# A warm-up of TensorE in small tiles, in a retention-and-hardswish kernel on one core

## The chip, the core and the metric

The kernel runs on one core of a Trainium2 chip. The core has TensorE (PE, with its weight loads shown apart as PEld), VectorE (DVE), ScalarE (ACT), GpSimd (POOL) and SyncE (SP), and sixteen DMA engines ("rings" below, one queue's share of a transfer on each). The metric is device time in microseconds of one execution, a median over several. The time before is 289.05 us, the median of three runs from 288.21 to 289.22.

## The reference

Two stages, one after the other. The first is a retention layer: for 8 batches and 8 heads, sequence 576, head size 64,

```python
scores = scale * np.matmul(q, k.transpose(0, 1, 3, 2))
Dmat = np.where(rel >= 0, gamma[:, None, None] ** rel[None, :, :], 0.0)   # rel = s - t, gamma by head
ret = scores * Dmat[None, :, :, :]
attn_out = np.matmul(ret, v)
```

The second takes the 4608 x 512 result as x and runs a feed-forward layer with w_in (512 x 2048) and w_out (2048 x 512):

```python
h = x @ w_in
g = h * np.clip(h + 3.0, 0.0, 6.0) / 6.0
out = g @ w_out
```

Inputs and output are float32; the kernel multiplies in float16 and accumulates in float32.

## The kernel before

The sequence is cut into pieces of 128 positions (four "main" pieces a batch and a shared "rest"). Retention runs piece by piece in chunked form: inside a piece by masked scores (`sc`, then `at` after the mask), across pieces by a state per head (`tbd`, `u`). The result `xt` goes, in blocks of 512 positions, through the first product (`ph`, with `win`), the hardswish on ACT and DVE, and the second product (`pout`, later in seven partial products `x`, `y`, `z`). From about 18 us on TensorE works through these products, with the retention of later pieces between them.

The order of the instructions on each engine is the order in which the program issues them (a manual schedule); engines meet by semaphores only. Everything that this change touches is at the beginning:

- SP loads q of pieces 0 and 1 in float32 (`load_q`, L123). POOL's queue then takes k and v of pieces 0 and 1, then q, k, v of pieces 2 and 3 (all L102), then `win` (L129) and `wout` (L134). These loads change float32 to float16 on the way, in packets of 128 bytes. Each transfer is split over sixteen rings, and a consumer waits for all sixteen parts.
- DVE sets up constants: `zeros` (L148, 128 x 512 float16), `cb` (L150, L151), the decay tables, the identity, and `dq` (L174), a diagonal matrix with the decay.
- TensorE starts with the warm-up: matmuls of `zeros` by `zeros` whose results nobody reads (`warm`, L215). Seven have 512 columns and two have 128. They write banks of the ring of four PSUM banks tagged `ph`.
- Then `q_by_pe(0)` (L265) brings q of piece 0 into transposed form with the decay (it needs ACT's cast of q, L126), `warm(2, MBLK)` follows, `k_by_pe(0)` (L256) transposes k, and `warm(6, P)` follows.
- For pieces 0 to 3 (the `EARLY` ones) come: scores (L341, the last piece L283), mask on DVE (L345, the last piece L286), the state (L314, L318 on TensorE, L323 on DVE), the output (L359 and L370, the last piece L297 and L303). `scale_v` (L245, DVE) scales v of each piece ahead of the state's matmul L314.
- The first block's first product starts behind piece 3's output with L600 (halves of 256 columns) and goes on with L574 (512 columns).

TensorE's and the other engines' instructions come from memory themselves; the profile shows their transfers as queues of the kind "instruction" (q8 in packets of 16 KB, q14 in packets of 8 KB).

The warm-up as it stands, and its call:

```python
    def warm(n, cols):
        w = bank([P, MBLK], FP32, name=f"warm_{warmed[0]}")
        warmed[0] += 1
        for _ in range(n):
            nc.tensor.matmul(w[:, 0:cols], zeros[:, 0:P], zeros[:, 0:cols],
                             start=True, stop=True)

    warm(7, MBLK)
    warm(2, P)
```

Of the kernel before, what the change touches and what calls it, by code (L numbers as in the profile page):

```python
# [10 lines left out]
FP32 = mybir.dt.float32  # L11
FP16 = mybir.dt.float16
# [5 lines left out]
def kernel(  # L18
# [16 lines left out]
    nc = tc.nc  # L35
# [3 lines left out]
    P = 128  # L39
    NPAIR = H // 2  # L40
    HALF = P // 2
    NCC = DM // P
    NFC = DFF // P
    MBLK = 512
# [18 lines left out]
    const = ctx.enter_context(tc.tile_pool(name="const", bufs=1))  # L63
# [21 lines left out]
    def bank(shape, dtype, name):  # L85
        return psum.tile(shape, dtype, tag="ph", bufs=4, name=name)
# [8 lines left out]
    def load_third(c, i):  # L95
        if c not in loaded:
            vn = nat.tile([P, H, D], FP16, tag="vn", bufs=NBUF, name=f"vn_{c}")
            qk = nat.tile([P, 2, H, D], FP16, tag="qkn", bufs=NBUF, name=f"qkn_{c}")
            loaded[c] = {"qkn": qk, "q16": qk[:, 0], "kn": qk[:, 1], "vn": vn, "dma": []}
        dst, src = ((loaded[c]["kn"], k), (loaded[c]["q16"], q), (loaded[c]["vn"], v))[i]  # L100
        for p0, b, s0, n in pieces[c][3]:
            loaded[c]["dma"].append(nc.gpsimd.dma_start(  # L102
                dst[p0:p0 + n], src[b, :, s0:s0 + n, :].rearrange("h s d -> s h d")))
# [9 lines left out]
    def load_kv(c):  # L113
        load_third(c, 0)
        load_third(c, 2)
# [28 lines left out]
    load_q(1)  # L144
    load_kv(0)
    load_kv(1)
    zeros = const.tile([P, MBLK], FP16)
    nc.vector.memset(zeros, 0.0)  # L148
    cb = const.tile([P, 2], FP32)
# [51 lines left out]
    for i in range(5):  # L201
# [2 lines left out]
            nc.vector.memset(t, 0.0)  # L204
        tbd.append(t)

    newest = [None]
    warmed = [0]

# [5 lines that stand above are left out]
            nc.tensor.matmul(w[:, 0:cols], zeros[:, 0:P], zeros[:, 0:cols],  # L215
                             start=True, stop=True)

    warm(7, MBLK)
    warm(2, P)

    def make_mask64():
# [8 lines left out]
    free_tbd = list(range(5))  # L230
    state_of = {}
    ts_of = {}

    def rows(i):
        return slice(i * HALF, i * HALF + HALF)

    def run_later(n):
        for _ in range(n):
# [159 lines left out]
    def update_state(c, copies_later=False):  # L398
# [14 lines left out]
        if last:  # L413

            state_of[b] = None
            ts_of[b] = lambda h2, p: ts[rows(h2), p, :]
        else:
            new = free_tbd.pop(0)
            state_of[b] = new
# [19 lines left out]
    def scores4(cs):  # L439
        sc = psum.tile([P, 2, 2, NPAIR, HALF], FP32, tag="sc", name=f"sc_{cs[0]}")  # L440
        at = work.tile([P, 2, 2, NPAIR, HALF], FP16, tag="at", bufs=3, name=f"at_{cs[0]}")
        for j, c in enumerate(cs):
            qk = st[c]["qk"]
            st[c]["at"] = at[:, :, j]
            for p in range(NPAIR):
                for h2 in range(2):
                    for half in range(2):
                        nc.tensor.matmul(sc[rows(half), h2, j, p, :],  # L448
                                         qk[rows(h2), 1, p, rows(half)],
                                         qk[rows(h2), 0, p, rows(half)], start=True, stop=True)  # L450

        def mask():
            if len(cs) == 2:
                nc.vector.tensor_tensor(  # L454
                    out=at.rearrange("t a j p s -> t (a j p) s"),
                    in0=sc.rearrange("t a j p s -> t (a j p) s"),
                    in1=mask64[:, None, :].to_broadcast([P, 4 * NPAIR, HALF]), op=ALU.mult)
            else:
                nc.vector.tensor_tensor(
                    out=at[:, :, 0], in0=sc[:, :, 0],  # L460
                    in1=mask64[:, None, None, :].to_broadcast([P, 2, NPAIR, HALF]), op=ALU.mult)
        return mask
# [626 lines left out]
```

## Time and profile before

| what | value |
|---|---|
| median of three runs | 289.05 us (288.21 to 289.22) |
| profiled execution | 288.14 us |
| its span, first to last instruction | 286.4 us |
| TensorE busy | 277.3 us (97%) |
| DVE, ACT, POOL busy | 227.9, 177.5, 107.2 us |
| warm-up matmuls on the timeline | 1.20 to 4.58 us |
| first matmul of the first product (L600) | 18.11 us |

The span starts with the first instruction and all times below are counted from it; 1.7 us of the execution lie outside. In lines of the timeline the first number is the start, the second the time until the last of the merged instructions ends, and in brackets the idle time before it with what ended it. In the table by stretches, each engine has its busy time and its number of instructions in brackets, then the granted TensorE clock, the DMA share and GB/s. The column of the granted clock has no records for the first microseconds and shows 1.00 there; the spacing of matmuls tells the clock instead.

### The profile page before, as it was taken

What the parts mean: (1) busy time and instruction counts of PE and PEld (TensorE: products, weight loads), DVE (VectorE), ACT (ScalarE), POOL (GpSimd) and SP (SyncE); (2) the same over time, 40 slices, a digit from 0 to 9 for tenths busy, and PEclk for the clock granted to TensorE, in tenths of its full rate; (3) what the DMA queues carried; (4) which work ended last, traced back from release to release, by engine and by line L of the source; (5) the groups of instructions that cost most, each with busy time, mean ns of one, the idle gap of its engine ahead of it and who ended that gap; (6) DMA issues with size and microseconds to landing.
All of it is one profiled execution on the core that took longest, in us unless ns stands there. A gap on an engine that the chain in (4) does not pass through costs nothing.

```text
span 286.4 us, 8439 instructions
## 1 busy us (share of the span) xinstructions
PE 277.3 (97%) x3540; PEld 178.8 (62%) x3540; DVE 227.9 (80%) x376; ACT 177.5 (62%) x313; POOL 107.2 (37%) x134
## 2 busy tenths in 40 slices
PE   7879999999999999999999999999999999999994
PEld 3544445864565597459745884588458845874583
DVE  4948756898768998899879997999799678727861
ACT  6748437875458655865587557755775477358720
POOL 8962669266404332432443434256640000000000
PEclk9999999999999999999999999999999999999999
DMA  9999999999999979998999999999993240121014
GB/s 138 153 195 205 190 160 217 178 151 163 134 169 165 128 81 128 161 150 83 123 172 154 72 132 177 161 78 126 179 157 48 79 108 5 39 76 38 3 37 110
DMA packets 156166, 35.94 MB, mean 125 GB/s; under 512 B 142912, under 2 KB 155072, under 8 KB 156128
## 3 DMA queue, kind: packets, MB, share of 16 engines
q0 software_dynamic: 115760, 18.23, 89.8%
q1 hardware_dynamic: 39920, 16.78, 28.4%
q8 instruction: 27, 0.44, 0.6%
q10 hardware_dynamic: 448, 0.39, 0.4%
q14 instruction: 11, 0.09, 0.1%
HBM read 36.70 MB, written 9.44 MB: 161 GB/s over the span
## 4 chain that ended last, share of the span: by engine, by line
PE 92%; POOL 3%; DMA 2%; DVE 1%; issue 0%; ACT 0%; POOLq 0%
PE ph L574 39%; PE x L712 15%; PE pout L627 10%; PE z L712 9%; PE y L712 4%; PE ph L600 4%; DMA vn<-in_v_dram 2%; POOL qkn L102 2%; PE sc L448 2%; PE o L480 2%; PE o L502 2%; PE u L530 1%; PE xtu L712 1%; PE xo L712 1%; POOL vn L102 1%; PE o L370 1%
## 5 line engine op out<-in xcount | busy, mean ns | idle before, releaser
L574 PE MATMUL ph<-xt,win 128*128 128x512 f16 x520 | 113.7, 379 | 0.0
L582 ACT ACTIVATE u<-ph,cb 128x512 f32<-128x512 f32 x130 | 89.3, 687 | 23.2 <-PE ph L574 23.0
L583 DVE SCALAR_TENSOR_TENSOR gt<-u,ph 128x512 f16<-128x512 f32 x130 | 87.0, 685 | 17.7 <-ACT u L582 16.3
L574 PEld LDWEIGHTS <-win 128*128 128x128 f16 x520 | 50.9, 98 | 59.4
L102 POOL DMA_DIRECT2D qkn<-in_k_dram x40 | 34.0, 850 | 47.6 <-PE ph L600 16.8
L712 PEld LDWEIGHTS <-sum_s 128*128 128x128 f16 x448 | 43.2, 98 | 5.5 <-issue 0.3
L102 POOL DMA_DIRECT2D vn<-in_v_dram x40 | 33.9, 848 | 25.7 <-PE ph L574 10.9
L102 POOL DMA_DIRECT2D qkn<-in_q_dram x38 | 32.1, 845 | 29.9 <-PE ph L574 8.5
L712 PEld LDWEIGHTS <-gt 128*128 128x128 f16 x336 | 32.5, 98 | 5.4
L627 PE MATMUL pout<-wout,gt 128*128 128x512 f16 x128 | 29.1, 379 | 0.0
L680 POOL DMA_DIRECT2D out_dram<-osb x1 | 0.6, 617 | 68.2 <-DVE osb L733 68.2
L712 PE MATMUL x<-wsum_t,sum_s 128*128 128x256 f16 x192 | 22.9, 273 | 0.0
L627 PEld LDWEIGHTS <-gt 128*128 128x128 f16 x128 | 12.0, 98 | 13.5
L330 DVE TENSOR_TENSOR qkn<-qkn,gqk 128x1024 f16<-128x1024 f16 x28 | 19.1, 683 | 0.0
L668 DVE TENSOR_TENSOR sum_s<-gt 128x1024 f16<-128x1024 f16 (+1 forms) x21 | 18.1, 864 | 0.2
L454 DVE TENSOR_TENSOR at<-sc,mask 128x1024 f16<-128x1024 f32 x14 | 17.0, 1217 | 1.1 <-PE sc L448 1.1
L514 ACT CAST xt<-o 64x512 f16<-64x512 f32 x28 | 16.2, 580 | 0.3
L564 DVE TENSOR_TENSOR ta<-u,th 128x256 f32<-128x256 f32 x24 | 10.2, 424 | 5.4 <-ACT th L549 4.4
L712 PE MATMUL z<-wout,sum_s 128*128 128x256 f16 x112 | 13.6, 273 | 0.1
L712 PE MATMUL z<-wsum_t,sum_s 128*128 128x256 f16 x112 | 13.5, 273 | 0.0
L712 PE MATMUL y<-wout,gt 128*128 128x256 f16 x112 | 13.4, 273 | 0.0
L600 PE MATMUL ph<-xt,win 128*128 128x256 f16 x112 | 12.9, 273 | 0.0
(122 smaller groups left out, 304.4 us busy)
## 6 DMA issues: line engine op xcount, KB each, us to landing
out_dram<-osb SPq DMA_DIRECT2D x32, 256.0 KB, 3.6
qkn<-in_k_dram POOLq DMA_DIRECT2D x32, 128.0 KB, 5.1
vn<-in_v_dram POOLq DMA_DIRECT2D x32, 128.0 KB, 5.2
qkn<-in_q_dram POOLq DMA_DIRECT2D x30, 128.0 KB, 5.5
wout<-in_moe_w_out_dram POOLq DMA_DIRECT2D x4, 512.0 KB, 14.8
win<-in_moe_w_in_dram POOLq DMA_DIRECT2D x4, 256.0 KB, 7.6
win<-in_moe_w_in_dram POOLq DMA_DIRECT2D x2, 512.0 KB, 11.2
qf<-in_q_dram SPq DMA_DIRECT2D x2, 256.0 KB, 3.5
```

The source lines that it names most:

```text
L102: loaded[c]["dma"].append(nc.gpsimd.dma_start(dst[p0:p0 + n], src[b, :, s0:s0 + n, :].rearrange("h s d -> s h d")))
L330: nc.vector.tensor_tensor(out=both, in0=both, in1=gqk, op=ALU.mult)
L454: nc.vector.tensor_tensor(out=at.rearrange("t a j p s -> t (a j p) s"), in0=sc.rearrange("t a j p s -> t (a j p) s"), in1=mask64[:, None, ...
L514: nc.scalar.copy(to[rows(h2), :, :, 1, :], o[1][rows(1 - h2)].rearrange("e j p s -> e p j s"))
L564: nc.vector.tensor_tensor(out=ta, in0=st[c]["u"][1], in1=st[c]["sum"], op=ALU.add)
L574: newest[0] = nc.tensor.matmul(ph, win16[:, dmc, P * fc:P * fc + P], xt_of(kb)[:, dmc, :], start=(dmc == 0), stop=(dmc == NCC - 1))
L582: nc.scalar.activation(u, ph, ACTF.Relu, bias=cb[:, 0:1], scale=1.0 / 6.0)
L583: nc.vector.scalar_tensor_tensor(out=gts[kb][:, fc, :], in0=u, scalar=1.0, in1=ph, op0=ALU.min, op1=ALU.mult)
L600: newest[0] = nc.tensor.matmul(ph[:, i], win16[:, dmc, P * (fc + i):P * (fc + i) + P], xt_of(kb)[:, dmc, cols], start=(i == 0 and dmc == 0 ...
L627: nc.tensor.matmul(pout, gt[:, fc, P * mc:P * mc + P], wout16[:, fc, :], start=(fc == 0), stop=(fc == NFC - 1))
L668: nc.vector.tensor_tensor(out=s(which)[:, c0:c1], in0=x(), in1=y(), op=op)
L712: newest[0] = nc.tensor.matmul(dst, left()[:, c, P * u:P * u + P], right[:, c, :], start=(first and c == 0 and (u == 0 or name not in whol ...
```

## The change

A tile `few` of 128 x 64 float16 zeros is set ahead of `zeros`. The seven matmuls of 512 columns give way to 113 small ones and two of 512. A small one multiplies 64 rows of `few` by 64 rows of `few`, 64 columns, and writes one half of the partitions of one of two PSUM banks; four in a row use the four quarters of TensorE's array in turn. The two of 128 columns stay. The helper `rows` moves up in the program unchanged.

```diff
     load_kv(0)
     load_kv(1)
+    few = const.tile([P, HALF], FP16)
+    nc.vector.memset(few, 0.0)
     zeros = const.tile([P, MBLK], FP16)
     nc.vector.memset(zeros, 0.0)
...
+    def rows(i):
+        return slice(i * HALF, i * HALF + HALF)
+
...
-    warm(7, MBLK)
+    def warm_small(n):
+
+        w = [bank([P, MBLK], FP32, name=f"warm_small{x}") for x in range(2)]
+        for i in range(n):
+            x, h = divmod(i % 4, 2)
+            nc.tensor.matmul(w[x][rows(h ^ x), 0:HALF], few[rows(h)], few[rows(h)],
+                             start=True, stop=True)
+
+    warm_small(113)
+    warm(2, MBLK)
     warm(2, P)
...
-
-    def rows(i):
-        return slice(i * HALF, i * HALF + HALF)
```

## The prediction

> **What bounds the kernel now.** I read the page first (busy shares, DMA queues), then the chain of waits, then the timeline of the first 20 us, because the change touches nothing later. The page, shares and DMA queues:
> ```profile
> span 286.4 us, 8439 instructions
> PE 277.3 (97%) x3540; PEld 178.8 (62%) x3540; DVE 227.9 (80%) x376; ACT 177.5 (62%) x313; POOL 107.2 (37%) x134
> ...
> q8 instruction: 27, 0.44, 0.6%
> ```
> TensorE is the bound, and the busy time by stretches says where it is not: 12.01 us busy of the first 16.67, then 29.00 of 29.00.
> ```profile
> 0.00:16.67 16.67, 12.01 (x143) 6.70 (x143) 10.43 (x36) 10.51 (x23) 14.78 (x23) 1.00 1.85 150
> ...
> 84.00:113.00 29.00, 29.00 (x442) 21.11 (x441) 27.15 (x45) 19.76 (x36) 9.97 (x12) 1.00 1.04 118
> ```
> So from the first L600 matmul on, the end follows at a fixed distance, and the change is worth what it does to the start of L600, now 18.11 us. The timeline of the beginning:
> ```profile
> 1.20 3.38 PE L215 MATMUL warm<-zeros 128*128 128x512 f16 x9 [1.20 <-DVE cb L150]
> ...
> 3.93 0.62 ACT L126 CAST qkn<-qf 128x512 f16<-128x512 f32 x1 [1.40 <-DMA qf<-in_q_dram]
> ...
> 4.60 0.64 PE L265 MATMUL trq<-dq,qkn 128*64 128x128 f16 x8
> ...
> 14.47 0.40 PE L283 MATMUL sc<-qk 64*128 64x128 f16 x8
> ...
> 16.20 0.43 DVE L245 TENSOR_TENSOR vn<-vn,gqk 128x512 f16<-128x512 f16 x1 [1.96 <-DMA vn<-in_v_dram]
> ...
> 16.54 1.28 DVE L286 TENSOR_TENSOR at<-sc,mask_wide 128x512 f16<-128x512 f32 x2
> 16.68 0.23 PEld L314 LDWEIGHTS <-qkn 128*128 128x128 f16 x4 [1.99 <-DVE vn L245]
> 16.68 0.40 PE L314 MATMUL u<-vn,qkn 128*128 128x128 f16 x4 [1.82 <-DVE vn L245]
> ```
> (q8: packets, MB, share.) See that the first real work (L265) waits for q's cast, which waits for a DMA, and not for the warm-up; and that TensorE later stands 1.82 us for the scaled v of the fourth piece, whose load is late. The chain of waits and the queues in the 10 ns after 14.10 us:
> ```profile
> 9.35 6.83 DMA vn<-in_v_dram
> ```
> ```profile
> q8 instruction: 1, 0.02, 592.5%
> ```
> That load took 6.83 us where the other early ones took 4.6 to 4.9. In the trace's records fifteen of its sixteen parts had landed by 13.98 us and the last at 16.18; in between, at 14.107, one 16 KB packet of q8 ran for 0.95 us, and the last two packets of v went right after it, at 15.04. q8 moves 27 packets for the 7080 instructions of TensorE (262 each), and this first one starts when 268 of them are counted in the stretch 0 to 14.11 us. I read it as TensorE's own instructions being fetched through a ring that still held v.
>
> **The change, part by part.** *Start of the warm-up.* The small matmuls wait for the memset of `few`, 32 words a partition against 256 for `zeros`. The zeros memset took 0.27 us, one of one word 0.06; in between by size, 0.09 us. TensorE started 0.05 us after the memset, so it starts at 0.87 + 0.09 + 0.05 = 1.01 in place of 1.20. DVE's later setup moves by up to 0.09 us; dq (L174) waits 0.33 us for ACT, which hides it. If not, it would cost at most 0.09.
>
> *113 small matmuls.* The trace has such 64x64 tiles at full clock only:
> ```profile
> 66.61:66.87 0.27, 0.26 (x32) 0.27 (x1) 0.15 (x1) 1.00 1.88 188
> ```
> 32 in 0.27 us, 8.3 ns each, four tiles at a time. The warm-up runs at the slow clock: L215 starts every 0.427 us there against 0.228 at 5.17 us, and the L265 pairs every 0.106 us at 4.60 against 0.056 at 7.85. At 1.9 times, 15.8 ns each, 1.79 us. Bounds: 113 x 8.3 = 0.94 us, and one after another at half of 0.106 us, 6.0 us. I take 1.79, the nearest rows being the same tiles. With two of 0.427 and two of 0.106 (1.07 us) the warm-up ends at 1.01 + 1.79 + 1.07 = 3.87 us, against 4.37 now. L265 waits for the cast that ends at 4.55 either way: no gain. At the upper bound L265 would be 3.5 us late. Bank numbers turn by two in the ring of four; the tiles that they wait for are long done, 0 us.
>
> *Where TensorE's instructions are counted.* 117 matmuls with their weight loads in place of 9 add 216 instructions ahead of everything. What now begins as number 268 at 14.1 us will be number 484; number 268 becomes today's 52, which falls at about 6 to 7 us, and earlier if the issue runs ahead. So the first q8 packet comes in the span 4 to 7 us, and the second at today's number 308, about 17.2 us, behind the wait for v. The late v then has the pace of the other loads: 9.35 + 4.8 = 14.15 us.
>
> *What is late next.* With v there at 14.15, its scaling ends by 14.7, behind DVE's tbd (13.56 + 0.68). The scores at L283 (14.47) then set the pace: L345 follows its scores by 0.44 us, so L286 starts at 14.91 in place of 16.54 and L600 at 18.11 - 1.63 = 16.48 us. That is the most that can be won, 1.63 us. The packet has a price in its new place: 0.95 us on one ring that holds k and v of pieces 0 and 1. Of this k of piece 1 has 0.33 us to spare (landed 7.87, used 8.20), v of piece 0 has 0.15 (its scaling ends at 7.49, and DVE's next step L345 starts at 7.64), k of piece 0 nothing. Each of them starts the chain of DVE and TensorE work that ends at L286, and DVE is busy 3.91 of the 4 us from 8 to 12, so a delay stays: 0.62 to 0.95 us, I take 0.8. From below: nothing, if it falls before 3.9 us, where these queues are empty. From above: the 2.1 us that this packet cost v where it is now, and then 0.5 us are lost, not won. The lag left on v's ring is below the chain's delay. Later packets move by 216 instructions too; the view of waits names none of TensorE's after 18.2 us, so 0.
>
> *The clock.* The L215 rows show it turn between 4.93 and 5.17 us, 4.0 us after the first matmul. I take the same time after the change. TensorE's streaming there falls from 3.17 to 2.86 us and has a pause of 0.7 us ahead of L265, so this can fail. The Trainium skill, "TensorE: Matmul & The Clock Gate", Part 1, says the clock opens after a free-running window of about 3.4 us that was busy; a warm-up with a pause could by it miss one window, and the sum would be that of the second rival below in place of mine. The rows of before neither confirm nor refuse that.
>
> Sum: L600 at 16.48 + 0.8 = 17.3 us, 0.8 us less. The profiled execution took 288.14 us (span 286.4 and 1.7 around it), 0.9 below the median of 289.05 and below all three runs (288.21 to 289.22). From its own time 287.35, from the median 288.25; I say **287.8**, between them.
>
> **The rivals.**
> *Full gain.* The packet runs while the load queues are empty, before about 3.9 us, or in a slack. For it: the small matmuls are issued fast, and the count reaches 236 in the warm-up itself. Against: the first packet today came only at 268. L600 at 16.48: 288.14 - 1.63 = 286.5, or 287.4 from the median.
> *Nothing is won.* The packet costs the early loads its 2.1 us, or the clock needs another 4.0 us: from 5.17 to 9.2 the chain has six groups of 0.21 us (L256 twice, L341, L314, L265, L370) that take as long again, 1.26 us, and L600 starts at 17.3 + 1.26 = 18.56. 288.1 to 288.6; from the median up to 289.5. For it: the ring is at work without a break from 4 to 13 us (148 GB/s) and has little to catch up with. The Trainium skill, "Runtime: NRT & Kernel Launch", "Instruction fetch mechanics", has instructions come in blocks of 256 whose fetch is mostly hidden; by that this case gives 288.14 too. The count of 262 a packet agrees with it; the late v speaks against "hidden".
> *Slower: the clock stays slow into the dense part.* Place: TensorE from 5.17 us. The small tiles and the pause leave the clock closed; the waits up to 14 us may keep it so. Price: 25 groups of 0.21 us up to L600 take 5.3 us more, and with half to all of it on the chain L600 is at 16.48 + 2.65 to 5.3 = 19.1 to 21.8, plus some 2 us for 4 us of L600 and L574 at half speed: 291.1 to 293.8. It decides once over 3.1 us are lost (1.63 of cover and 0.5%). Against: TensorE was busy only 3.81 of the 6 us from 12 to 18, and the clock held.
>
> **How the numbers follow.** A measurement of this kernel tells some 0.5% (1.44 us) from no change, so faster means below 287.6. Forecast case, chance 0.42, 287.2 to 288.4 by its two bases: 0.15 of it faster, 0.27 the same. Full gain 0.20, faster. Nothing won 0.20, the same (it starts at 288.1, and ends 0.2% above the median). Slow clock 0.18, slower. Together faster 0.35, same 0.47, slower 0.18. The range reaches from the full gain (286.5) to short of the slow clock's cases (290.5).
>
> **What would show it.** The first q8 packet at 4 to 7 us and none at 13 to 16; DVE L245 of the fourth piece waiting under 0.5 us near 14 to 15 us; L600 starting at 17.3; L265 still at 4.60; 113 small ones in about 1.8 us; L215 and L256 after 5.2 us at the fast spacing (0.228 and 0.056). The prediction is wrong if the fourth v is late again, if the groups after 5.2 us keep the spacing of 0.106, or if TensorE waits for instructions.

## The result, and the profile after

The changed kernel takes 289.15 us (median of 11 runs, 287.99 to 289.56) against 287.21 for the kernel before (median of 11, 286.72 to 289.22). The ratio is 1.0052, with a 95% interval of 1.0029 to 1.0075: slower by about half a per cent, 0.8 to 2.2 us. The forecast was 287.8 and a small gain over 289.05. The time lies in the stated range of 286.5 to 290.5, but the kernel moved the other way. The three runs that were known of the kernel before (288.21 to 289.22) lie at the upper end of its spread: the eight others of this comparison took 286.72 to 287.39.

In the changed kernel the line numbers behind the warm-up are 11 higher: L265 is L276, L256 is L267, L245 is L256, L600 is L611.

The page of the changed kernel, its span, its instruction queue and the granted clock in 40 slices of 7.2 us:

```profile
span 287.2 us, 8657 instructions
...
PEclk9599999999999999999999999999999999999999
...
q8 instruction: 28, 0.46, 0.7%
```

The second slice, 7.2 to 14.4 us, ran at half clock (the digit of the first slice counts only from the first record, at 3.80 us). The timeline of the changed kernel's beginning (start, time to the end, work, idle time before it and what ended it):

```profile
0.96 1.75 PE L228 MATMUL warm_small<-few 64*64 64x64 f16 x113 [0.96 <-DVE few L148]
...
2.65 1.25 PE L220 MATMUL warm<-zeros 128*128 128x512 f16 x4
...
4.57 0.41 PE L276 MATMUL trq<-dq,qkn 128*64 128x128 f16 x8 [0.68 <-ACT qkn L126]
...
4.92 0.60 PE L220 MATMUL warm<-zeros 128*128 128x512 f16 x2
...
7.43 0.61 PE L267 MATMUL trk<-ident,qkn 128*128 128x128 f16 x4 [1.91 <-DMA qkn<-in_k_dram]
...
17.15 0.41 DVE L256 TENSOR_TENSOR vn<-vn,gqk 128x512 f16<-128x512 f16 x1
...
19.17 1.92 PE L611 MATMUL ph<-xt,win 128*128 128x256 f16 x16
```

The warm-up does what was worked out, and L276 is on time. Then TensorE stands 1.91 us for k of piece 0. The fourth v (the L256 step at 17.15) now waits for nobody. L611 starts at 19.17 us. The queues of the changed kernel in the 10 ns after 3.46 us, and the beginning of its chain of waits:

```profile
q8 instruction: 1, 0.02, 746.2%
```

```profile
1.37 6.02 DMA qkn<-in_k_dram
7.39 0.05 issue
7.43 0.61 PE trk L267 x4
```

The first packet of instructions has moved from 14.1 to 3.46 us, where it runs for 1.19 us. Fifteen of the sixteen parts of k of piece 0 had landed by 5.96 us, the last at 7.39. The last part of each of the next seven loads is 1.4 us behind the fifteenth as well, up to 13.7 us. The profile does not name the ring of a packet; that this one shares a ring with the late part is read from the times. They agree in all fourteen profiles: in the eight whose first packet comes by 5.8 us, k or v of piece 0 has one part that lands 1.2 to 1.8 us behind the fifteenth, and in the six others none of the two is over 0.3 us behind.

The same stage of the kernel before in a second profiled execution, of 286.93 us:

```profile
6.22 0.40 PE L256 MATMUL trk<-ident,qkn 128*128 128x128 f16 x4
...
14.35 0.43 DVE L245 TENSOR_TENSOR vn<-vn,gqk 128x512 f16<-128x512 f16 x1
...
16.69 1.92 PE L600 MATMUL ph<-xt,win 128*128 128x256 f16 x16
```

Its first packet runs from 13.17 us, v of the fourth piece lands at 14.32 all the same, and L600 starts at 16.69, not at 18.11. So the comparison is 19.17 against 16.69, 2.48 us. TensorE's work and clock between k and the first product, by stretches, of the changed kernel and then of the kernel before:

```profile
7.40:19.17 11.77, 11.07 (x141) 7.49 (x142) 8.18 (x12) 6.78 (x14) 10.79 (x15) 0.72 2.01 171
```

```profile
6.22:16.69 10.47, 8.81 (x141) 5.93 (x142) 8.34 (x12) 6.91 (x15) 10.00 (x13) 1.00 2.44 161
```

The same 141 matmuls, busy 11.07 us at a mean clock of 0.72 against 8.81 at 1.00. Of the 2.48 us, 1.21 is the later start of k's transposition (7.43 against 6.22), and 1.27 is the longer way from there (11.74 against 10.47). The dense part gives 0.38 us back (263.87 against 264.25 us from the first L600 or L611 to the last matmul); near 137 us this execution of the kernel before has 0.52 us between two starts of TensorE, and the changed kernel has no such gap. That leaves 2.10; the two executions differ by 2.06 us.

### The profile page after: what moved, and what is told of

It reads as the page before. It is cut to its first block, busy times and chain, and to the rows that moved or that the text cites. A ratio compares the mean times of both kernels' runs of the same rounds, so it can differ in the third digit from the quotient of the medians.

```text
span 287.2 us, 8657 instructions
## 1 busy us (share of the span) xinstructions
PE 278.7 (97%) x3648; PEld 181.0 (63%) x3648; DVE 228.3 (79%) x377; ACT 177.6 (62%) x313; POOL 107.2 (37%) x134
## 4 chain that ended last, share of the span: by engine, by line
PE 91%; DMA 5%; DVE 1%; ACT 1%; issue 0%; POOL 0%; POOLq 0%
PE ph L585 39%; PE x L723 15%; PE z L723 9%; PE pout L638 7%; PE y L723 4%; PE ph L611 4%; DMA qk<-qkn 3%; DMA qkn<-in_k_dram 2%; PE o L513 1%; PE sc L459 1%; PE o L491 1%; PE xtu L723 1%; PE xo L723 1%; PE u L541 1%; PE sc L352 1%; PE trq L276 1%
## 5 line engine op out<-in xcount | busy, mean ns | idle before, releaser
L594 DVE SCALAR_TENSOR_TENSOR gt<-u,ph 128x512 f16<-128x512 f32 x130 | 87.0, 685 | 17.3 <-ACT u L593 16.0
L611 PE MATMUL ph<-xt,win 128*128 128x256 f16 x112 | 12.9, 273 | 0.0
## 6 DMA issues: line engine op xcount, KB each, us to landing
wout<-in_moe_w_out_dram POOLq DMA_DIRECT2D x4, 512.0 KB, 14.9
```

Source lines behind the costliest of these rows:

```text
L594: nc.vector.scalar_tensor_tensor(out=gts[kb][:, fc, :], in0=u, scalar=1.0, in1=ph, op0=ALU.min, op1=ALU.mult)
L611: newest[0] = nc.tensor.matmul(ph[:, i], win16[:, dmc, P * (fc + i):P * (fc + i) + P], xt_of(kb)[:, dmc, cols], start=(i == 0 and dmc == 0 ...
```

## The experiments

Two causes stood against each other: the *transfer* (216 more instructions bring the first packet forward onto the rings that hold k and v) and the *clock* (small tiles and a pause warm TensorE badly). Runs of one group share the runs of the kernel before.

**The changed kernel again.**

> The changed kernel as it is, to see how its start varies. Theory 'transfer': the first 16 KB packet of TensorE's instructions again comes at 3 to 4 us, k of piece 0 lands after 7 us in place of 6.1, and L611 starts near 19 us; 1.0 to 1.9 us over the kernel before. Theory 'clock': the delay is the slow clock; then executions differ with the time at which the clock opens, and one with a clock that stays open from 3.8 us on has L611 before 18 us, with the packet where it is.

Measured: 289.02 us, ratio 1.0057 (1.0036 to 1.0077). Packet at 4.36 us, last part of k at 7.66, L267 at 7.70, L611 at 18.50. The full clock is on record from 4.42 to 7.83 us and again from 11.24. The transfer is confirmed. That L611 comes before 18 us when the clock opens early is not, but the clock did not stay open either: it closed just after the wait for k.

**The count alone.** The full array, as many instructions:

```diff
-    warm(7, MBLK)
+    warm(115, P // 4)
     warm(2, P)
```

> The kernel before with its seven matmuls of 512 columns cut into 115 of 32 columns in the full 128x128 array: the instruction count of the change (234 against 18), about the same columns in all (3680 against 3584), no small tiles. Theory 'transfer': first packet at 3 to 5 us, k of piece 0 about 1.3 us late, +1.0 to +1.5 us as with the change. Theory 'clock': the array is filled as before, so within 0.3 us of the kernel before.

Measured: 288.68 us, ratio 1.0039 (1.0021 to 1.0057). The packet came at 5.80 us, too late to hold k of piece 0 (landed at 6.17, on time); v of piece 0 landed at 8.51, 1.5 us behind its fifteenth part. The waits of this kernel:

```profile
DVE vn L245 <- DMA vn<-in_v_dram: 3.4, 1, 3.4
...
PE u L314 <- DVE vn L245: 1.4, 1, 1.4
```

So the instruction count by itself, with the array as full as before, brings most of the loss (1.3 us over the kernel before, where the changed kernel has 1.7 in the same group), and the rival that wanted 0.3 us at most falls. The clock comes in behind it: it closed from 8.88 to 15.71 us. Five of its ten runs have a mean recorded clock of 0.997 or more and took 287.44 to 288.57 us (mean 287.84); the five at 0.994 or less took 288.80 to 289.42 (mean 289.12). Where no closing is on record, the count costs only half a microsecond here.

**The shape alone.** Small tiles and pause, few instructions:

```diff
-            nc.tensor.matmul(w[x][rows(h ^ x), 0:HALF], few[rows(h)], few[rows(h)],
+            nc.tensor.matmul(w[x][rows(h ^ x)], few[rows(h)], zeros[rows(h)],
                              start=True, stop=True)
-    warm_small(113)
+    warm_small(14)
```

> The changed kernel with its 113 small matmuls of 64 columns merged into 14 of 512 columns in the same 64x64 tiles (the same columns, some 1.6 us, the same pause of about 0.7 us), so 36 instructions of warm-up in place of 234. Theory 'transfer': the first packet stays late (after 11 us), k of piece 0 lands at 6.1 us, within 0.3 us of the kernel before. Theory 'clock': small tiles and pause are the cause, so the clock opens late or closes again and +1.0 to +1.5 us as with the change.

Measured: 288.25 us, ratio 1.0023 (1.0003 to 1.0043). The packet stays at 12.96 us, k lands at 6.28, and L611 starts at 17.16, two microseconds sooner than in the changed kernel, although the clock opened only at 9.48. Neither expectation on the time is met: it is 0.9 us over the kernel before, and half of that comes from somewhere new. The waits of this kernel's TensorE from 136 to 140 us:

```profile
PE o L513 <- issue: 1.2, 1, 1.2
```

In the middle of a burst of small matmuls TensorE stands, with 1.42 us between two starts, and the profile names no engine and no load. A packet of q8 ran from 136.13 to 137.06 us, and TensorE went on 1.4 us after its end. In the kernel before the longest distance of two starts there is 0.36 and 0.52 us in the two profiles, in the changed one 0.20.

**The pause filled.** Four matmuls of 512 columns behind the small ones:

```diff
-    warm(2, MBLK)
-    warm(2, P)
+    warm(4, MBLK)
```

> The changed kernel with four matmuls of 512 columns after the small ones in place of two of 512 and two of 128, so that the pause of 0.7 us ahead of L276 is filled and the count of instructions stays 234. Theory 'transfer': no gain, k of piece 0 is still late, +1.0 to +1.5 us over the kernel before. Theory 'clock': the clock opens and stays open, and the time falls back to the kernel before or under it.

Measured: 288.77 us, ratio 1.0059 (1.0042 to 1.0076). Packet at 4.21, k at 7.62, L611's place at 18.59; the clock open from 6.06 to 9.47 and again from 12.89. Filling the pause wins nothing, though it left some idle time ahead of L276 (0.29 us in place of 0.68). So the pause was not the cause of the loss.

**The kernel before again.**

> The kernel before, unchanged, for a profile of its usual execution (the one shown took 288.1 us, eight later ones 286.7 to 287.4). Theory 'v is usually in time': the first packet of instructions falls beside v of piece 3 without holding it, v lands near 14.2 us and L600 starts near 17 us. Theory 'v is always late': L600 at 18 us, and the later executions are faster for a reason elsewhere.

Measured: 287.60 us, ratio to its own other runs 1.0008 (0.9993 to 1.0024). Its profile is the one shown above: v of piece 3 is in time, and L600 starts at 16.69 us. Over all groups the kernel before has medians of 287.21, 287.37, 287.29 and 287.93 us, with single runs from 286.65 to 290.14; the execution of 288.14 us that the prediction was read from is one of the longer ones. That all the longer ones have a late v is not shown: only these two were profiled.

**The packet sooner.** 16 columns in the small matmuls:

```diff
-            nc.tensor.matmul(w[x][rows(h ^ x), 0:HALF], few[rows(h)], few[rows(h)],
+            nc.tensor.matmul(w[x][rows(h ^ x), 0:16], few[rows(h)], few[rows(h), 0:16],
                              start=True, stop=True)
...
     warm_small(113)
-    warm(2, MBLK)
+    warm(5, MBLK)
```

> The changed kernel with 16 columns in place of 64 in the small matmuls, and five of 512 in place of two after them: the count of instructions is nearly the same (240 against 234), but they are used up faster, so that the first packet should come some 0.7 us sooner, about 2.7 to 3.7 us, when the rings do not yet hold k. Theory 'transfer': the last part of k of piece 0 lands 0.4 to 1.0 us sooner than with the change (6.3 to 7.0), and the time falls by 0.5 to 1.2 us, to 0 to +1.0 us of the kernel before. Theory 'clock': the warm-up is now mostly the old one, so the clock opens and stays as in the kernel before and the time falls by all of it, whatever the packet does.

Measured: 289.12 us, ratio 1.0061 (1.0041 to 1.0081). The edit failed to do what it was for: 113 matmuls of 16 columns take as long as of 64 (the next work starts at 2.60 in place of 2.65 us), and the packet came at 4.51 us. The changed kernel itself has it at 3.46, 4.36 and 3.93 in three profiles, so its place varies by more than the edit was to move it. As a test of the place it says nothing. As a second look at the clock it is clear: k at 7.91, clock closed from 8.62 to 15.45, L611 at 19.74.

**The wait for k filled, first try.** In the changed kernel:

```diff
     q_by_pe(0)
-    warm(2, MBLK)
+    warm(8, MBLK)
```

> The changed kernel with eight matmuls of 512 columns in place of two between L276 and L267, so that TensorE has work while k of piece 0 is late. Theory 'the late k closes the clock, and the slow clock adds to it': k lands late as before, but the clock does not close after it, the groups up to L611 keep the spacing of 0.056 us, and L611 starts 0.5 to 1.0 us sooner than with the change; +0.3 to +1.0 us over the kernel before. Theory 'the late transfer alone': no gain over the change, +1.5 us.

Measured: 288.59 us, ratio 1.0047 (1.0022 to 1.0073). Inconclusive: in the profiled execution the clock opened for the first time at 9.94 us, so the eight matmuls, at half clock, outlasted the wait for k (landed at 7.61), and L267 started only at 8.80. From there to L611 it took 10.29 us, as in the kernel before (10.47).

**The wait for k filled, second try.** The same edit on the kernel with 16 columns:

> The kernel with 16 columns in the small matmuls and five of 512 after them (packet at 4.5 us, L611 at 19.74, clock open at 5.21 and closed again from 8.62 to 15.45), with eight matmuls of 512 columns in place of two between L276 and L267. Theory 'the late k closes the clock, and the slow clock adds to it': the clock opens by 5.2 us and stays open, k still lands near 7.9, and L611 starts at 18.0 to 18.5, the lateness of k alone (1.4 us) over the 16.7 of the kernel before; 0.5 to 1.5 us less than without the fill. Theory 'the late transfer alone': L611 stays near 19.5.

Measured: 287.80 us, ratio 0.9990 (0.9970 to 1.0011), against 1.0061 without the fill. The kernel before had slower runs in this group (median 287.93, elsewhere 287.21 to 287.37), so I compare the profiles. Without the fill, then with it:

```profile
7.95 0.40 PE L267 MATMUL trk<-ident,qkn 128*128 128x128 f16 x4 [1.89 <-DMA qkn<-in_k_dram]
...
19.74 0.50 PE L611 MATMUL ph<-xt,win 128*128 128x256 f16 x3
```

```profile
8.26 0.39 PE L267 MATMUL trk<-ident,qkn 128*128 128x128 f16 x4
...
18.30 1.92 PE L611 MATMUL ph<-xt,win 128*128 128x256 f16 x16
```

With the fill L267 starts 0.31 us later and L611 1.44 us sooner. The clock opened at 7.46 (later than I had expected) and did not close. The way from L267 to L611 is 10.05 us in place of 11.79. All ten runs with the fill have a mean recorded clock of 0.998 or more; without it seven of nine have 0.994 or less. This isolates the second half of the loss in this kernel: the wait for k lets the clock close, and the slow clock stretches the chain behind it.

**Small tiles once more, other places of the blocks.** The kernel with 14 small tiles, and 12 instructions fewer:

```diff
     warm(2, MBLK)
-    warm(2, P)
+    warm(1, 2 * P)
...
-    warm(6, P)
+    warm(1, MBLK)
```

> The 14 small tiles of 512 columns again, with 12 instructions fewer (two of 128 columns become one of 256, the six of 128 ahead of the scores one of 512), so that the blocks of instructions begin nearly where they do in the kernel before (6 later in the count in place of 18). Theory 'the stall of 1.4 us at 138 us came from the place of a block': it is gone, and the time falls by 0.7 to 1.2 us, to within 0.5 us of the kernel before, the rest being the clock that opens late. Theory 'small tiles are dear in themselves': +0.6 us as before.

Measured: 287.92 us, ratio 1.0003 (0.9976 to 1.0030). The time is as expected against the runs of its group (median 287.93, elsewhere 287.21 to 287.37), the reason is not: the stall near 138 us is still there with 1.02 us between starts. The clock opened at 5.02 us this time and L611 started at 16.65. So at the start small tiles cost nothing by themselves when the clock opens in time; the dense part behind is 0.9 us longer than in the second profile of the kernel before (265.17 against 264.25).

**Twelve instructions fewer in the kernel before**, twice:

```diff
     warm(7, MBLK)
-    warm(2, P)
+    warm(1, 2 * P)
...
-    warm(6, P)
+    warm(1, MBLK)
```

> The kernel before with 12 instructions fewer ahead of the first product: the two of 128 columns become one of 256, and the six of 128 ahead of the scores become one of 512. Every block of instructions begins 12 later. Theory 'places of the packets decide': the first packet comes 0.5 to 1 us later, after v of piece 3 has landed, and the time is 0 to 1 us under the kernel before. Theory 'they do not': the same within 0.3 us.

> The kernel before with 12 instructions fewer once more, in more rounds. If the places of the packets decide: first packet after 14.3 us, no stall near 138 us, 0.3 to 0.7 us under the kernel before. If not: the same within 0.2 us.

Measured: 286.87 us, ratio 0.9986 (0.9965 to 1.0008), then 286.68, ratio 0.9958 (0.9939 to 0.9978). The packet comes at 14.74 and 14.99 us, behind the fourth v; L600 starts at 16.56 and 16.83. The first profile has no gap near 138 us; the second has 0.76 us between two starts, where the expectation had none. The two medians are the lowest of all kernels here; the second interval lies below 1, but in the group in which the kernel before was slowest, and the first includes 1. It is the best version found, by 0.1 to 0.4%, and the reason (no execution with a late v) is argued from two profiles, not shown.

**The changed kernel a third time.**

> The changed kernel for a third profile. Its executions with a mean clock of 0.998 to 1.0 are no faster than those with 0.988 to 0.994. Theory 'the clock opens late in these': the first record of the full clock stands after 8 us, the packet at 3.4 to 4.4, L611 at 18.5 to 19.5. Theory 'the packet alone': the clock is open from 3.8 to 5.5 us on without a break, and L611 still starts after 19 us.

Measured: 289.06 us, ratio 1.0034 (1.0005 to 1.0063). Packet at 3.93 us, L267 at 7.60, L611 at 19.00. The mean clock of this profile is 0.999, but the first record of a full clock stands at 13.03 us. Its timeline shows the change of speed in the length of the groups:

```profile
12.36 0.61 PE L325 MATMUL u<-vn,qkn 128*128 128x128 f16 x4
12.76 0.52 PE L329 MATMUL u<-tbd,ident 128*128 128x512 f16 x1
13.21 0.41 PE L276 MATMUL trq<-dq,qkn 128*64 128x128 f16 x8
```

Four matmuls take 0.61 us at the slow and 0.40 at the full clock, eight of L276 0.64 and 0.41. So a mean clock near 1 does not say that TensorE was fast from the beginning: ahead of the first record nothing counts.

This bears on the first profile of the changed kernel. Of this kernel's 23 executions in the three groups, only six have a mean recorded clock of 0.994 or less, which is what one closing of 3.4 us leaves of 287; the 17 others have 0.998 or more and are no faster (median 289.25 us against 288.57). Of the 17 only the execution above has a profile, and in it the clock opened late. That the others have a late opening too is likely, not shown.

All fourteen profiles together (us; "chain" is from the first transposition of k, L256 or L267, to the first product, L600 or L611):

| kernel | first packet | k of piece 0 landed | k's transposition | first product | chain | full clock on record |
|---|---|---|---|---|---|---|
| before, as shown | 14.11 | 6.07 | 6.12 | 18.11 | 11.99 (v late) | from 5.21 |
| before again | 13.17 | 6.18 | 6.22 | 16.69 | 10.47 | from 5.77 |
| twelve fewer | 14.74 | 6.20 | 6.25 | 16.56 | 10.31 | from 4.49 |
| twelve fewer again | 14.99 | 6.43 | 6.48 | 16.83 | 10.35 | from 6.55 |
| tiles, 14 | 12.96 | 6.28 | 6.32 | 17.16 | 10.84 | from 9.48 |
| tiles, 14, twelve fewer | 13.70 | 6.33 | 6.38 | 16.65 | 10.27 | from 5.02 |
| changed | 3.46 | 7.39 | 7.43 | 19.17 | 11.74 | 3.80 to 7.21, from 14.04 |
| changed again | 4.36 | 7.66 | 7.70 | 18.50 | 10.80 | 4.42 to 7.83, from 11.24 |
| changed, third | 3.93 | 7.56 | 7.60 | 19.00 | 11.40 | from 13.03 |
| wait for k filled, first try | 4.20 | 7.61 | 8.80 | 19.09 | 10.29 | from 9.94 |
| count alone, full array | 5.80 | 6.17 | 6.21 | 19.51 | 13.30 (v of piece 0 late) | 5.47 to 8.88, from 15.71 |
| pause filled | 4.21 | 7.62 | 7.67 | 18.59 | 10.92 | 6.06 to 9.47, from 12.89 |
| 16 columns | 4.51 | 7.91 | 7.95 | 19.74 | 11.79 | 5.21 to 8.62, from 15.45 |
| 16 columns, wait filled | 3.65 | 7.22 | 8.26 | 18.30 | 10.05 | from 7.46 |

## Why the prediction was wrong, step by step

*Start and length of the warm-up.* Right: start 0.96 us (1.01 worked out), the 113 small matmuls to 2.65 (2.80), the end of the warm-up within 0.1 us of 3.87 (the last merged row starts at 2.65 and lasts 1.25), L276 at 4.57 and not held by it. The small matmuls were a little quicker than foretold: from the first to the last their starts lie 13.6 ns apart, where 1.9 times the 8.3 ns of the full clock gave 15.8.

*Where the instructions are counted.* Right in its mechanism and nearly in its place: the first packet came at 3.46 us (4 to 7 foretold, and "earlier if the issue runs ahead"), the second at 18.73 (17.2). That the move frees the fourth v is right too: it landed at 14.71.

*"That is the most that can be won, 1.63 us."* This is the step that failed. It took the late v of the one profiled execution for the kernel's standing state. In the second profiled execution the same packet runs at 13.2 us beside the same load, and v is at hand at 14.3; the chain that I worked out for the case "v in time" (L600 at 16.48 us) is what the kernel then already does (16.69). In such an execution there is nothing to be won, and the cover of 1.63 us, behind which a delay of the early chain was to vanish, is not there. It is not the whole miss: L611 came at 19.17 us, 1.9 later than the 17.3 foretold and 1.06 later than even the 18.11 of the kernel before with a late v. Of these 1.9 us, 1.27 are the clock, a term that the sum put at nothing, 0.4 the price of the packet and 0.2 the chain with v in time. So the cover and the clock each were enough to turn the small gain into a loss. That 289.15 still lies in the range is luck: the range was drawn around a kernel before of 288.14 to 289.05, and that kernel's median is 287.21. The hint lay in the numbers: runs that spread over 1 us, where a packet's place against a load could be a matter of tenths.

*The price in the new place, "I take 0.8".* Mis-sized: k of piece 0 landed 1.21 us later (1.0 to 1.7 over the kernels whose packet came at 3.5 to 4.5 us), above the stated 0.62 to 0.95 and under the upper bound of 2.1. It hit k of piece 0, which has nothing to spare, and it was dearer than the 0.95 us that the packet lasted in the kernel before: here it ran for 1.19 us, and the part that it held came 1.43 us behind the others.

*The clock, "I take the same time after the change".* Of the three profiles two have the clock open by 5.2 us as foretold (at 3.80 and 4.42) and one only at 13.03. Wrong is what the term left out: once k is late TensorE idles, and in both of the two the clock that had opened closes for one or two stretches of 3.4 us. One stretch costs 0.3 to 0.5 us of chain, two cost 1.3 (10.80 and 10.92, 11.74 and 11.79 against 10.47).

*The rivals.* "Nothing is won" had the two right mechanisms, a late k and a chain at half clock, and for the second nearly the right price (1.26 against 1.27 us; for the first 2.1 against 1.21), but as alternatives and against a start of 18.11; they came together, against 16.69. "Slower" named the right engine and the right place, with a clock that stays slow into the dense part; the clock was back by 14 us, and the loss (2.06 us between the profiles) stayed below its lowest price (3.0). The Trainium skill, "TensorE: Matmul & The Clock Gate", Part 1, has the clock judged in windows of about 3.4 us; the recorded stretches (3.80 to 7.21, 7.21 to 14.04) are one and two times 3.41 us, so the trace agrees. The Trainium skill says in the section on HAM oscillation of the same page that a wait for a load throttles the engine again and the work behind it runs cold. The trace agrees that this happens (the clock closed at 7.21 us, in a wait that began at 5.5), but not with the length: the section has idle gaps of over some 3.4 us do it, and here a wait of 1.91 us was enough. The prediction left this way from a late k to the clock out. "Runtime: NRT & Kernel Launch" of the Trainium skill, "Instruction fetch mechanics", calls the fetch mostly hidden; here it was not, by the 1.21 us that k of piece 0 came later.

*What is settled and what is open.* That the count of instructions causes the late load is shown by the kernel that has the count and not the tiles, and by the two that have the tiles and not the count. That the slow clock adds to it is shown by the filled wait. Why the first opening comes at 3.8 us in one execution and at 13.0 in another of the same kernel is open. The pause ahead of L276 may have a part in it: without the pause (the kernel with it filled and the one with 16 columns) 11 of 13 executions have a closing on record, which needs an early opening, and with it 6 of 23; the time lost is the same. What the small tiles do to the clock is open as well: the five profiles without them have the first opening at 4.49 to 6.55 us, the nine with them at 3.80 to 13.03, four of these after 7 us. And the count alone cost half a microsecond where no closing is on record, while the 17 executions of the changed kernel without one lost over 1 us; that may be the late opening or the load that the packet hits (v of piece 0 there, k here).

## What to carry to other kernels

Instructions are loads too: each 256 or so of TensorE's cost one 16 KB packet of about 1 us on a ring that, by the times here, also carries data, so the number of dummy instructions at the start decides which load is held up. Before a stall is counted as a gain to be had, look at more than one execution: a wait in one profile may be missing in the next, and with it goes the cover that seemed to hide other costs. And follow a late load to the clock: the idle time it makes may cost as much again behind it.

## What the runs showed of the hardware that was not expected

- A packet of TensorE's instructions lasted 0.88 to 1.92 us over all profiles. Behind the early one, one part of each load stayed 0.9 to 1.8 us behind the others (1.4 in the changed kernel) through the seven or eight loads that landed up to some 14 us.
- The granted clock closed for one or two stretches of 3.41 us in or after a wait of 1.4 to 2.0 us for k or v near the start (five profiles; in the changed kernel 1.91 us, TensorE busy 0.95 of the 2.86 us from 4.57 to 7.43), but held through 1.8 us without work from 14.9 to 16.7 us in the kernel before.
- 64x64 tiles by 16 columns are hardly faster than by 64 in the warm-up: from the first of the 113 to the next matmul behind them it took 1.64 and 1.69 us.
- TensorE stood for 1.2 us in the dense part with no engine and no load named, and went on 1.4 us after the end of a packet of its own instructions (at 138.5 us, the kernel with 14 small tiles). That it had run out of instructions is an inference.
